# Three edits to a fused attention, soft-MoE and MLP kernel: values' remainder later in the load queue, expert weights two rows per partition, a narrower opening matmul

## The chip, the cores and the metric

The kernel runs on one core of one Trainium2 chip, in float32 with the float32r format in the last stage. The metric is the time of one execution on the device in microseconds. Before the change three runs gave 629.23 to 629.75 us, median 629.69 us. The profiled execution is another one: it took 630.9 us, of which 629.1 us lie between its first and last instruction (the span).

## What is computed

Three layers follow each other, each on the whole output of the one before.

```
# 1. packed attention, 8 batches x 8 heads, 576 tokens of 64, 32 pack queries
p_packed = softmax(p @ k.T / 8) @ v            # 32 x 64 for each head
x = softmax(q @ p_packed.T / 8) @ p_packed     # 576 x 64 for each head, then 4608 x 512
# 2. soft MoE, 8 experts of 4 slots
logits = x @ phi
slots = softmax(logits, over tokens).T @ x     # 32 x 512
slot_out[e] = relu(slots[e] @ w1[e]) @ w2[e]   # w1: 512 x 1024, w2: 1024 x 512
x = softmax(logits, over slots) @ slot_out     # 4608 x 512
# 3. MLP with Mish
out = mish(x @ w_in) @ w_out                   # 512 -> 2048 -> 512
```

The softmax over tokens needs every batch, so the first expert product can't start before the attention of the last batch has ended.

## The kernel before, in words

**Loads.** All loads of q, k, v and of the weights are issued by SyncE (SP), in one order that is fixed when the program is written: the list `jobs` (lines 61 to 214). A job is one load into a named place: a half batch (4 heads) of k or q (576 KB, one DMA), a half batch of v (512 KB, four DMAs of 128 KB, line 129), or 512 KB of weights. `plan` gives each job its place among 29 places for the attention's data, later 37 places of 512 KB; `pump` emits jobs in order, and each DMA waits on SP until the last reader of what lay in its place before is done. SP executes in order, so a load that waits holds up all loads behind it. Up to eight loads of this queue are in flight: each of its DMAs takes the completion semaphore of the one eight DMAs before it and waits for that one to land.

The first 57 jobs, counted from 0, are: k, v, q of batch 0 and k of batch 1 (0 to 7), p (8), then for b = 0, 1, ...: k of batch b+2, v of batch b+1, q of batch b+1, two jobs each. So v of batch 2 is jobs 17 and 18, its q 19 and 20, k of batch 4 is 21 and 22, v of batch 3 is 23 and 24, and so on; k of batch 6 is jobs 33 and 34. Jobs 49 to 56 are the first eight tiles of w_in, and from 57 on come the expert weights, w1 and w2 of four tiles each for every expert, with more w_in tiles among them and sixteen w_out tiles at the end (129 to 144).

**The remainder of v.** A head has 576 = 18 x 32 tokens. Sixteen of the 18 rows of each group of tokens come with job v; the other two, of all eight heads, come as a tile of their own, `vr` (64 partitions, two DMAs of 64 KB in pieces of 256 bytes, line 139), with the second job of that batch's v. There are two buffers of `vr`, so those of batch b wait until the matmuls `pv` of batch b-2 have read theirs.

**Attention.** A loop written out by hand (lines 770 to 817) overlaps three batches: in the pass of b it has the second softmax of b, the product with v of b+1 (`pv`, line 415) and the first softmax of b+2. Each engine executes its instructions in that order. In `pv` the matmuls of a half batch take the sixteen main rows first and the remainder last (line 427).

**Experts.** `ex_h` computes slots @ w1 of an expert, `ex_x` turns its result to put hidden rows on partitions (four matmuls with the 0/1 matrix `idm`, then a 32x32 transpose on VectorE), `ex_o` multiplies with w2. Tile c of w2 holds rows 256c to 256c+255; partition p holds row 256c+p in its first half and row 256c+128+p in its second. The very last tile comes as two DMAs, one for each half. Between the attention and this, the first eight w_in tiles are converted (`bg`), which frees their places for jobs 81 to 93.

**MLP.** 18 blocks of 256 tokens, each in four steps over the hidden dimension. Blocks 5 to 17 form the second product by a scheme with seven products of half size (`emit_o`, lines 1349 to 1368) that add into the PSUM banks Z, V, W, U, X, Y. Bank W holds two sums side by side, 256 columns each. Its first matmul of a block is written over all 512 columns, with a moving operand (`TT["open"]`) whose second half is zeros, so that both halves start from a fresh sum.

Of the kernel before, what the change touches and what calls it, by code (L numbers as in the profile page):

```python
# [9 lines left out]
F32 = mybir.dt.float32  # L10
# [9 lines left out]
def kernel(  # L20
# [13 lines left out]
    nc = tc.nc  # L34
    B, H, S, D = q.shape
    J = p.shape[2]
    E, DM, F1 = w1.shape
    M = phi.shape[1]
# [3 lines left out]
    HQ = H // 4  # L42
# [18 lines left out]
    jobs = []  # L61
# [11 lines left out]
    def plan():  # L73

        late = len(AFTER[E - 1, 1])
        a, x = [("a", i) for i in range(RA)], [("x", i) for i in range(RX)]
        first = [(z, 18 * D * i) for z, n in (("y", 2), ("c", 4), ("w", 16)) for i in range(n)] + a
        order.extend(first[(i - N_QKV) % len(first)] for i in range(N_QKV))
        y, c, w = ([(z, 1024 * i) for i in range(n)] for z, n in (("y", RY), ("c", RC), ("w", RW)))
        again = c[0:1] + w[0:4] + c[1:] + w[8:12] + w[4:8] + w[12:]  # L80
        order.extend((y + c + w + x + a + again + w[0:4] + w[8:12] + w[4:8])[0:len(jobs) - late - N_QKV] + (a + x + a[2:5] + x)[0:late])
# [27 lines left out]
    def take(*name):  # L109
        if name not in got:  # L110
            pump()
        return got[name]
# [10 lines left out]

    vr_t = {}

    def job_v(b, hq):
        def emit(t):
            for h4 in range(4):
                nc.sync.dma_start(
                    out=t[:, 4 * h4 * D:4 * h4 * D + 4 * D],  # L130
                    in_=v[b, 4 * hq + h4].rearrange("(r j) d -> r (j d)", j=18)[:, 0:16 * D].rearrange(
                        "r (a x) -> r a x", a=4,
                    ),
                )
            if hq == HQ - 1:
                vr = t1.tile([64, H, D], F32, name="vr", tag="vr", bufs=2)
                vr_t[b] = vr
                for i in range(2):
                    nc.sync.dma_start(
                        out=vr[32 * i:32 * i + 32], in_=v[b].rearrange("h (r j) d -> r j h d", j=18)[:, 16 + i],  # L140
                    )
        return emit

    def job_w1(e, c):
# [3 lines left out]

    def job_w2(e, c):
        def emit(t):  # L150
            if (e, c) == (E - 1, 3):
                for f in range(2):
                    r = 256 * c + 128 * f
                    nc.sync.dma_start(out=t[:, DM * f:DM * f + DM], in_=w2[e, r:r + 128, :])
                return
            nc.sync.dma_start(
                out=t[:, 0:2 * DM].rearrange("p (f n) -> p f n", f=2),
                in_=w2[e, 256 * c:256 * c + 256, :].rearrange("(f p) n -> p f n", p=128),
            )
        return emit  # L160

# [18 lines left out]
    def add_qkv(nm, b):  # L180
        for hq in range(HQ):
            jobs.append(((nm, b, hq), job_v(b, hq) if nm == "v" else job_kq(k if nm == "k" else q, b, hq)))
# [29 lines left out]
    add_cv((E - 1, 1))  # L212
    assert len([j for j in jobs if j[0][0] in ("wi", "wo")]) == 32
    plan()


    t1 = p1.enter_context(tc.tile_pool(name="t1", bufs=2))
    one = p1.enter_context(tc.tile_pool(name="one", bufs=1))
# [472 lines left out]
    def r_last(b):  # L691
# [13 lines left out]
        out=pT[:, 0:2 * HQ].rearrange("p a c j -> p (a c j)"), in_=p_s.rearrange("p a c -> p (a c)"),  # L705
# [20 lines left out]
        out=pT[:, 2 * HQ:].rearrange("p a c j -> p (a c j)"), in_=take("p")[:, 0:(B - 2) * HQ * D],  # L726
# [223 lines left out]
    for hq in range(HQ):  # L950
        for z in range(2):
            nc.tensor.matmul(
                sit_ps[64 * z:64 * z + 64, 64 * hq:64 * hq + 64].rearrange("p (g m) -> p g m", g=2),
                lhsT=si_acc[:, 64 * hq:64 * hq + 64], rhs=ident.rearrange("p (g z m) -> p z g m", g=2, z=2)[:, z],
                start=True, stop=True,
# [15 lines left out]
    ex = {}  # L971
    idm = t2.tile([128, 512], F32, name="idm", tag="msb")[:, 0:E * (M + SPE)]
    nc.gpsimd.memset(idm, 0.0)
    nc.gpsimd.tensor_copy(
        out=idm.rearrange("p (e x) -> p e x", e=E)[:, :, 0:SPE], in_=ids.rearrange("p (e s) -> p e s", s=SPE),
# [22 lines left out]

    def ex_x(e):

        h1 = ex[e][0].rearrange("p (k c j) -> p k c j", c=4, j=32)
        xp = ps_x.tile([128, FT1, M], F32, name="xp", tag="x")
        for c in range(4):
            nc.tensor.matmul(
                xp[32 * c:32 * c + 32], lhsT=idm[:, M * e:M * e + M], rhs=h1[:, :, c], start=True, stop=True,
            )
        h1T = two.tile([128, FT1, M], F32, name="h1T", tag="h1T")
        nc.vector.transpose(out=h1T.rearrange("p k m -> p (k m)"), in_=xp.rearrange("p k m -> p (k m)"))
        nc.vector.tensor_scalar_max(out=h1T, in0=h1T, scalar1=0.0)
        ex[e][1] = h1T  # L1010
# [71 lines left out]
    ex_h(0)  # L1082
    ex_h(1)
    ex_x(0)
    ex_h(2)
    ex_x(1)
    cb = combine(0)
    next(cb)
    ex_o(0)
    ex_x(2)  # L1090
    ex_h(3)
    ex_o(1)
# [40 lines left out]
    blk = {}  # L1133
# [37 lines left out]
    def fast(n, c):  # L1171

        return not PLAIN.get(n, 0) >> c & 1
# [21 lines left out]
    R = {}  # L1195
# [49 lines left out]
    TT = {}  # L1245

    def wparts(c):
        return whi[:, 4 * c:4 * c + 4], wlo[:, 4 * c:4 * c + 4]
# [70 lines left out]
    def emit_o(n, c, mid):  # L1319

        last = c == ORDER[n][-1]
        H, L = wparts(c)
        x = blk.pop(("g", n, c))

        def mm(bank, o, lhsT, rhs, stop):
            first = (n, bank) not in blk
            blk[n, bank] = True
            nc.tensor.matmul(o, lhsT=lhsT, rhs=rhs, start=first, stop=stop)  # L1328

        mixed = n in PLAIN  # L1330
        if not fast(n, c):
            gh, gl = x
            if (n, c) == (0, 0):
                for w, (g, b, fs) in enumerate(((gh, H, range(4)), (gh, L, range(2)), (gl, H, range(4)), (gh, L, range(2, 4)))):
                    for z, bank in enumerate("XY"):
                        for f in fs:
                            mm(bank, acc(n, bank), g[:, f, 128 * z:128 * z + 128], b[:, f], False)
                    if w > 1:
                        mid(2 * w - 4)
                return  # L1340
            for z, (tt, bank) in enumerate([(0, "X"), (1, "Y")][::-1 if n > 2 and c == ORDER[n][0] else 1]):
                for a, b in ((gh, H), (gh, L), (gl, H)):
                    for f in range(4):
                        mm(bank, acc(n, bank), a[:, f, 128 * tt:128 * tt + 128], b[:, f], last and a is gl and f == 3)
                if not z:
                    mid(0)
                    mid(2)
            return
        gh, gl, Sh, Sl = x
        A = lambda i, j: tuple(g[:, 2 * j:2 * j + 2, 128 * i:128 * i + 128] for g in (gh, gl))  # L1350
        S = lambda k: (Sh[:, k], Sl[:, k])
        Bw = lambda i, j: tuple(w[:, 2 * i:2 * i + 2, 256 * j:256 * j + 256] for w in (H, L))
        T1, T2, T3, T4 = TT[c]
        prods = (
            ("Z", 0, A(0, 0), Bw(0, 0)), ("V", 0, S(1), T2), ("W", 0, S(2), T3), ("X" if mixed else "W", 1, S(3), Bw(1, 1)),
            ("U", 0, S(0), T1), ("Y", 0, A(1, 1), T4), ("X", 0, A(0, 1), Bw(1, 0)),
        )
        for z, (bank, half, (ah, al), (bh, bl)) in enumerate(prods):
            o = R[bank][:, 256 * half:256 * half + 256]
            for f in (1, 0):  # L1360
                if bank == "W" and not mixed and (n, bank) not in blk:
                    mm(bank, R[bank].rearrange("p (z n) -> p z n", z=2), ah[:, f], TT["open"], False)
                else:
                    mm(bank, o, ah[:, f], bh[:, f], False)
                mm(bank, o, ah[:, f], bl[:, f], False)
            for f in (1, 0):
                mm(bank, o, al[:, f], bh[:, f], last and f == 0 and (bank, half) not in (("X", 1), ("W", 2 * mixed)))
            mid(z)
# [116 lines left out]
    for i, (n, c) in enumerate(steps):  # L1485
# [10 lines left out]
        def mid(z):  # L1496
            if z == 0 and last_s:
                nc.scalar.copy(out=quads(n)[1], in_=rq("Z"))
            if z == 1 and last_s:
                add(quads(n)[2], quads(n)[1], rq("V"))  # L1500
            if z in (0, 2) and nx:
                emit_h(*nx, z // 2)
                if i == 0:
                    m = 2 + z // 2
                    blk["mr", m] = bank("XY"[z // 2] + "2")
                    emit_mr(m, blk["mr", m])
# [8 lines left out]
        if i < N0:  # L1515
            cvt(CVT[i][0])
        emit_o(n, c, mid)
        if i == 0:
            cvt("u4 m4")
# [47 lines left out]
```

## Time and profile before

| what | value |
|---|---|
| median of three runs | 629.69 us (629.23 to 629.75) |
| profiled execution, its span | 630.9 us, 629.1 us |
| PE busy | 600.3 us (95%), 5874 matmuls |
| DVE busy | 499.9 us (79%) |
| ACT busy | 339.6 us (54%) |
| POOL busy | 47.9 us (8%) |
| read from HBM, written | 79.23 MB, 9.44 MB |
| chain that ended last | PE 66%, DVE 18%, DMA 8%, ACT 5% |

How to read it: the engines work side by side, so busy shares don't add up to the span, and the span has stages with different limits: attention to about 162 us, experts to about 216 us, the MLP to the end. Matmuls are pipelined, so a busy PE may still be waiting for operands. The chain of waits goes back from the last instruction, at each step to what released it; its shares say which engine the end depended on.

### The profile page before, as it was taken

Reading aid. Unit: us, or ns where it says so; the run is one execution under the profiler, and the core shown is the slowest. Engines: PE = TensorE matmul, PEld = TensorE weight load, DVE = VectorE, ACT = ScalarE, POOL = GpSimd, SP = SyncE. Lnnn points to the kernel's source line nnn. Section 1 sums busy time; section 2 is a strip of 40 time slices with the busy share of each in tenths; the row PEclk is TensorE's granted clock in tenths of the full one; section 3 lists DMA queues with packets and bytes.
Section 4 is the critical chain, followed back from the end, with each engine's and each line's share of the span. In section 5 each row is a group of like instructions: output and inputs, shape, how many; then the busy total and the mean of one; then the engine's idle time right before and its main releaser. Section 6 shows DMA issues by size and latency. Waiting matters only on the chain.

```text
span 629.1 us, 14397 instructions
## 1 busy us (share of the span) xinstructions
PE 600.3 (95%) x5874; PEld 518.4 (82%) x5874; DVE 499.9 (79%) x1004; ACT 339.6 (54%) x684; POOL 47.9 (8%) x73
## 2 busy tenths in 40 slices
PE   7799999998998999999999999999999999999997
PEld 5577777786434468888989899999999999999997
DVE  5998888978464388988999987788778878877883
ACT  3354555447334486666556555555555555555551
POOL 5122222112030000000000000000000000000000
PEclk9999999999999999999999999999999999999999
DMA  8998964999999961002110110111011101110100
GB/s 269 333 323 273 340 226 131 402 407 406 387 410 413 412 260 50 25 0 68 35 34 1 34 35 3 35 34 34 2 34 34 34 2 34 34 29 7 34 34 35
DMA packets 42162, 89.61 MB, mean 142 GB/s; under 512 B 10736, under 2 KB 19056, under 8 KB 42096
## 3 DMA queue, kind: packets, MB, share of 16 engines
q1 hardware_dynamic: 41696, 88.36, 39.5%
q8 instruction: 46, 0.75, 0.5%
q10 hardware_dynamic: 144, 0.26, 0.1%
q14 instruction: 20, 0.16, 0.1%
q0 software_dynamic: 256, 0.07, 0.1%
HBM read 79.23 MB, written 9.44 MB: 141 GB/s over the span
## 4 chain that ended last, share of the span: by engine, by line
PE 66%; DVE 18%; DMA 8%; ACT 5%; issue 1%; SPq 1%; DVEq 0%; POOL 0%; ACTq 0%; POOLq 0%
PE o L1328 45%; PE so L1328 8%; DMA AW<-in_moe_w_dram 7%; PE h L1205 5%; DVE kT L338 4%; DVE A L510 1%; DVE mx L509 1%; PE s L490 1%; DVE AY L1377 1%; DVE S L1221 1%; DVE sm L525 1%; ACT win L356 1%; DMA AC<-in_k_dram 1%; DVE nmx L386 1%; ACT AT L548 1%
## 5 line engine op out<-in xcount | busy, mean ns | idle before, releaser
L1328 PE MATMUL o<-W,gh 128*128 128x256 f32 (+1 forms) x648 | 119.2, 311 | 0.5 <-DVE AY L1377 0.5
L1236 ACT CAST gh<-AY 128x512 fp32r<-128x512 f32 x118 | 54.7, 511 | 111.6 <-PE o L1328 111.6
L1328 PE MATMUL o<-T,Sh 128*128 128x256 f32 x708 | 112.6, 281 | 1.8 <-DVE AY L1377 1.3
L1328 PEld LDWEIGHTS o<-W,gh 128*128 128x128 f32 x648 | 95.2, 188 | 7.8 <-issue 1.3
L1328 PEld LDWEIGHTS o<-T,Sh 128*128 128x128 f32 x708 | 95.7, 188 | 2.9 <-issue 1.1
L1210 ACT ACTIVATE AY<-h 128x512 f32<-128x512 f32 x126 | 74.2, 596 | 24.3 <-PE h L1205 23.3
L1239 DVE TENSOR_TENSOR gl<-AY,gh 128x512 fp32r<-128x512 f32 x118 | 60.5, 554 | 31.5 <-ACT gh L1236 31.5
L1240 DVE TENSOR_TENSOR Sl<-S,Sh 128x1024 fp32r<-128x1024 f32 x59 | 72.2, 1223 | 9.2 <-ACT Sh L1237 9.2
L1328 PE MATMUL o<-W,gl 128*128 128x256 f32 (+1 forms) x324 | 70.6, 310 | 0.0
L1328 PE MATMUL o<-T,Sl 128*128 128x256 f32 x354 | 69.7, 278 | 0.0
L1237 ACT CAST Sh<-S 128x1024 fp32r<-128x1024 f32 x59 | 61.9, 1049 | 7.7 <-DVE S L1221 7.7
L1328 PEld LDWEIGHTS o<-W,gl 128*128 128x128 f32 x324 | 52.4, 188 | 4.0
L1205 PE MATMUL h<-CS,W 128*128 128x256 f32 x288 | 55.4, 281 | 0.0
L1328 PEld LDWEIGHTS o<-T,Sl 128*128 128x128 f32 x354 | 53.8, 188 | 0.0
L1221 DVE TENSOR_TENSOR S<-AY 128x256 f32<-128x256 f32 x118 | 49.6, 420 | 5.2 <-ACT AY L1210 5.2
L1377 DVE TENSOR_TENSOR AY<-AY,o 128x256 f32<-128x256 f32 x115 | 45.1, 418 | 8.6 <-PE o L1328 4.8
L1205 PEld LDWEIGHTS h<-CS,W 128*128 128x128 f32 x288 | 44.0, 188 | 3.1 <-ACT s L1210 0.8
L1328 PE MATMUL so<-W,gh 128*128 128x256 f32 (+1 forms) x268 | 45.9, 294 | 0.0
L1328 PEld LDWEIGHTS so<-W,gh 128*128 128x128 f32 x268 | 37.8, 188 | 2.4 <-ACT W L1191 0.3
L376 PE MATMUL s<-kT,win 128*128 128x288 f32 x128 | 34.7, 414 | 4.7 <-ACT win L388 3.8
L1328 PE MATMUL o<-W,Sh 128*128 128x256 f32 x236 | 36.9, 278 | 0.0
L490 PE MATMUL s<-win,qT 128*128 128x128 f32 x256 | 32.1, 278 | 1.8 <-ACT win L356 1.8
(263 smaller groups left out, 989.2 us busy)
## 6 DMA issues: line engine op xcount, KB each, us to landing
AW<-in_moe_w_dram SPq DMA_DIRECT2D x45, 512.0 KB, 10.1
r_wo<-in_moe_w_out_dram SPq DMA_DIRECT2D x16, 512.0 KB, 8.9
out_dram<-AY SPq DMA_DIRECT2D x64, 128.0 KB, 2.1
r_wi<-in_moe_w_in_dram SPq DMA_DIRECT2D x13, 512.0 KB, 10.3
AW<-in_q_dram SPq DMA_DIRECT2D x11, 576.0 KB, 5.1
AW<-in_k_dram SPq DMA_DIRECT2D x9, 576.0 KB, 7.3
AW<-in_v_dram SPq DMA_DIRECT2D x40, 128.0 KB, 5.5
AC<-in_moe_w_dram SPq DMA_DIRECT2D x10, 512.0 KB, 11.0
```

The source lines that it names most:

```text
L338: nc.vector.transpose(out=T[:, dh, main].rearrange("p (i r a) -> p a i r" if nm == "k" else "p (i a r) -> p a i r", i=4, a=4,), in_=x[:, 0 ...
L376: nc.tensor.matmul(ps[:, n, 0:288], lhsT=pBD[b % 2][:, hq, dh], rhs=kT[:, dh, 288 * n:288 * n + 288], start=(dh == 0), stop=(dh == 1),)
L490: nc.tensor.matmul(ps[:, k - lo], lhsT=d["qT", hq][:, dh, 64 + 128 * i:192 + 128 * i], rhs=ppBD[b % 2][:, hq, dh], start=(dh == 0), stop=( ...
L1205: nc.tensor.matmul(hp[:, 256 * f:256 * f + 256], lhsT=MS[:, 128 * ft:128 * ft + 128], rhs=CS[:, 256 * n:256 * n + 256], start=True, stop=True,
L1210: nc.scalar.activation(out=s, in_=hp.rearrange("p (f n) -> p f n", f=2), func=AF.Mish)
L1221: nc.vector.tensor_tensor(out=S[:, k], in0=x, in1=y, op=op)
L1236: nc.scalar.copy(out=gh[:, f, t], in_=s[:, f, t])
L1237: nc.scalar.copy(out=Sh, in_=S)
L1239: nc.vector.tensor_tensor(out=gl[:, f, t], in0=s[:, f, t], in1=gh[:, f, t].bitcast(F32), op=ALU.subtract)
L1240: nc.vector.tensor_tensor(out=Sl, in0=S, in1=Sh.bitcast(F32), op=ALU.subtract)
L1328: nc.tensor.matmul(o, lhsT=lhsT, rhs=rhs, start=first, stop=stop)
L1377: add = lambda o, x, y: nc.vector.tensor_tensor(out=o, in0=x, in1=y, op=ALU.add)
```

## The change

It has three parts. The two DMAs of `vr` of batches 2 to 7 are issued not with the second v job of that batch but 15 jobs later, just ahead of that job's own DMA; the number of buffers is the same. Tile c of w2 is read with rows 256c+2p and 256c+2p+1 on partition p, 4 KB that lie together in memory, with one DMA also for the last tile; `ex_x` reads the columns of its operand two apart to match. And the first matmul into bank W has 256 columns, as the others.

```diff
+    def load_vr(b):
+        vr = t1.tile([64, H, D], F32, name="vr", tag="vr", bufs=2)
+        vr_t[b] = vr
+        for i in range(2):
+            nc.sync.dma_start(
+                out=vr[32 * i:32 * i + 32], in_=v[b].rearrange("h (r j) d -> r j h d", j=18)[:, 16 + i],
+            )
...
-            if hq == HQ - 1:
-                vr = t1.tile([64, H, D], F32, name="vr", tag="vr", bufs=2)
-                ...
+            if hq == HQ - 1 and b < 2:
+                load_vr(b)
...
     def job_w2(e, c):
-            if (e, c) == (E - 1, 3):
-                for f in range(2):
-                    r = 256 * c + 128 * f
-                    nc.sync.dma_start(out=t[:, DM * f:DM * f + DM], in_=w2[e, r:r + 128, :])
-                return
             nc.sync.dma_start(
-                out=t[:, 0:2 * DM].rearrange("p (f n) -> p f n", f=2),
-                in_=w2[e, 256 * c:256 * c + 256, :].rearrange("(f p) n -> p f n", p=128),
+                out=t[:, 0:2 * DM], in_=w2[e, 256 * c:256 * c + 256, :].rearrange("(p f) n -> p (f n)", f=2),
             )
...
     plan()
-
+    names = [j[0] for j in jobs]
+    for b in range(2, B):
+        i = names.index(("v", b, HQ - 1)) + 15
+        jobs[i] = jobs[i][0], lambda t, b=b, emit=jobs[i][1]: (load_vr(b), emit(t))
...
     def ex_x(e):
-        h1 = ex[e][0].rearrange("p (k c j) -> p k c j", c=4, j=32)
+        h1 = ex[e][0].rearrange("p (k c j f) -> p k f c j", c=4, j=32, f=2)
...
-                xp[32 * c:32 * c + 32], lhsT=idm[:, M * e:M * e + M], rhs=h1[:, :, c], start=True, stop=True,
+                xp[32 * c:32 * c + 32], lhsT=idm[:, M * e:M * e + M], rhs=h1[:, :, :, c], start=True, stop=True,
...
             for f in (1, 0):
-                if bank == "W" and not mixed and (n, bank) not in blk:
-                    mm(bank, R[bank].rearrange("p (z n) -> p z n", z=2), ah[:, f], TT["open"], False)
-                else:
-                    mm(bank, o, ah[:, f], bh[:, f], False)
+                mm(bank, o, ah[:, f], bh[:, f], False)
```

## Rows read from the trace of the kernel before

**Rows 1.** Page, 40 slices of the span: granted clock of TensorE.
```profile
PEclk9999999999999999999999999999999999999999
```

**Rows 2.** Timeline of SP, 33.9 to 62 us: start, us, engine, line, operation, out<-in, count.
```profile
34.06 1.54 SPq L139 DMA_DIRECT2D vr<-in_v_dram  x2
...
46.31 1.03 SPq L139 DMA_DIRECT2D vr<-in_v_dram  x2
...
57.67 1.60 SPq L139 DMA_DIRECT2D vr<-in_v_dram  x2
59.72 0.82 SPq L121 DMA_DIRECT2D AC<-in_q_dram  x2
60.65 0.43 SPq L121 DMA_DIRECT2D AC<-in_k_dram  x1
```

**Rows 3.** DMAs issued from 57.6 to 61.7 us: count, KB each, median us to landing.
```profile
AC<-in_q_dram SPq DMA_DIRECT2D x2, 576.0 KB, 4.9
...
vr<-in_v_dram SPq DMA_DIRECT2D x2, 64.0 KB, 3.1
```

**Rows 4.** Timeline of PE, 44 to 56 us.
```profile
49.02 0.32 PE L428 MATMUL pv<-vr,e1T 64*32 64x64 f32 x8
...
50.57 2.21 PE L376 MATMUL s<-kT,win 128*128 128x288 f32 x8 [0.40 <-ACT win L388]
```

**Rows 5.** Timeline of DVE, 44 to 58 and 73 to 91 us.
```profile
52.44 0.25 DVE L443 STREAM_TRANSPOSE ppT<-pp 128x128 f32<-128x128 f32 x1
...
57.79 0.17 DVE L395 TENSOR_SCALAR r<-sm 128x2 f32<-128x2 f32 x1 [1.71 <-ACT e L388]
...
74.98 0.17 DVE L395 TENSOR_SCALAR r<-sm 128x2 f32<-128x2 f32 x1 [1.71 <-ACT e L388]
```

**Rows 6.** Waits of SP's queue: us in total, times, longest.
```profile
SPq L139 <- PE pv L428: 13.7, 2, 10.2
...
SPq L129 <- DMA AW<-in_k_dram: 6.7, 7, 1.8
```

**Rows 7.** Timeline of SP, 100 to 165 us: waits end and loads go out.
```profile
102.19 0.93 SPq L139 DMA_DIRECT2D vr<-in_v_dram  x2
...
160.94 0.38 SPq L156 DMA_DIRECT2D r_w<-in_moe_w_dram  x1
164.19 0.38 SPq L156 DMA_DIRECT2D AC<-in_moe_w_dram  x1
```

**Rows 8.** Landing times of three single loads, issued at 160.94, 164.19, 233.24 us.
```profile
r_w<-in_moe_w_dram SPq DMA_DIRECT2D x1, 512.0 KB, 8.4
...
AC<-in_moe_w_dram SPq DMA_DIRECT2D x1, 512.0 KB, 6.5
...
r_wo<-in_moe_w_out_dram SPq DMA_DIRECT2D x1, 512.0 KB, 3.6
```

**Rows 9.** Windows: busy us of PE, PEld, DVE, ACT, POOL; PEclk, DMA share, GB/s.
```profile
142.00:162.00 20.00, 16.62 (x243) 12.66 (x232) 15.99 (x44) 12.18 (x36) 3.89 (x6) 1.00 1.03 402
...
192.00:202.00 10.00, 8.57 (x164) 4.56 (x160) 3.35 (x8) 3.53 (x8) 0.00 (x0) 1.00 1.03 416
204.00:213.00 9.00, 8.78 (x122) 4.10 (x122) 2.97 (x8) 3.35 (x7) 0.00 (x0) 1.00 1.05 408
```

**Rows 10.** Chain of waits, 160 to 220 us: start, us, what.
```profile
171.11 0.48 PE xp L1004 x8
...
203.85 10.14 DMA AW<-in_moe_w_dram
```

**Rows 11.** Timeline of PE, 370.4 to 377 us: a 512-column opening and the next step's.
```profile
370.46 0.75 PE L1328 MATMUL o<-T,Sh 128*128 128x512 f32 x4
...
376.00 0.64 PE L1328 MATMUL o<-T,Sh 128*128 128x256 f32 x4
```

**Rows 12.** Line 1328, PE: count, ns min/median/max, first and last start, forms.
```profile
L1328 PE MATMUL o<-T,Sh x708: 276/278/475, 295.7 to 622.8; 128*128 128x256 f32 x164, 128*128 128x512 f32 x13
```

**Rows 13.** Window at the end, columns as in Rows 9.
```profile
624.00:630.00 6.00, 0.66 (x6) 0.47 (x5) 1.14 (x4) 0.00 (x0) 0.00 (x0) 0.77 0.23 87
```

More of the change, by code (lines that the diff above doesn't have):

```diff
@@ L134, in emit @@
                 )
-            if hq == HQ - 1:
-                vr = t1.tile([64, H, D], F32, name="vr", tag="vr", bufs=2)
[L137 to L141, printed above, removed]
+            if hq == HQ - 1 and b < 2:
+                load_vr(b)
         return emit
```

## The prediction, made before the changed kernel ran

> **What bounds the kernel now.** I read the page first, then the chain of waits in order of time, then the timelines of SP, PE and VectorE (DVE) around the edits. The chain has three stretches. Up to 162 us it changes every microsecond or two between DVE, ScalarE (ACT) and PE and hardly ever reaches a DMA: the attention is bound by its own work, one pass of its loop in 17.2 us (the same DVE instruction at 57.79 and 74.98 us [rows 5]). From 172 to 214 us the chain is four loads of expert weights end to end, of which one is shown [rows 10]; the DMA engines are full there, and already in the last 20 us of the attention [rows 9]. From then on it is PE, almost without a gap, to the end. The granted clock is full in every slice [rows 1].
>
> **Remainder of v, the load queue.** In the attention SP waits 13.7 us in two places for `pv` to give back a `vr` buffer, 10.2 us of them before the load of the last batch at 102.19 [rows 6, 7], and all later loads stand behind it. The change takes these waits away. What it puts in their place I get by counting jobs. The second v job of batch 2 is job 18, so its `vr` now goes out ahead of job 33, the first load of k of batch 6. Before, job 33 was issued at 60.65 us [rows 2]. Three pairs of `vr` DMAs no longer stand ahead of it (batches 2, 3, 4): 1.54 and 1.03 us of SP, and 2.05 us from 57.67 to the next issue at 59.72, in all 4.6 us [rows 2]. So `vr` of batch 2 is issued at 56.0 us. Just ahead in the queue are the two halves of q of batch 4, issued 4.6 us earlier than before, at 55.1 and 55.5; such a load lands 4.9 us after its issue [rows 3], the second follows its fellow by about 1 us, and `vr` comes behind both. I estimate its landing at 61.3 us.
>
> `pv` of batch 2 begins its first `vr` matmul at 49.02 us [rows 4]. It will stand for 61.3 - 49.0 = 12.3 us. Behind it on PE are the first softmax of batch 3, which ran at 50.57 after 0.40 us of idling, and all that follows [rows 4]; ACT waits for the result of `pv`, and DVE for ACT, at the transpose that ran at 52.44 [rows 5]. The 0.40 us is slack; after it the delay passes to the pass as a whole: 11.9 us, and I take 11.6.
>
> Bounds for the landing: from the last v of batch 2 to `vr` lie 14 jobs, ten of 576 KB and four of 512 KB, 8.0 MB. At the highest rate that a window shows, 416 GB/s [rows 9], they need 19.2 us; starting at 34.06 us [rows 2] and with the 3.6 us that a load alone takes to land [rows 8] that is 56.9 us, a delay of 7.5 us. If the edit saves no issue time, 60.65 plus the 4.9 us of the loads ahead gives 65.6 us and a delay of 16.2 us.
>
> Can the attention win it back? In a pass DVE idles in one place, 1.71 us [rows 5], for an exponential of ACT that itself waits for DVE, so later passes have no slack to give. Five passes remain; if each gave all of that back, it would be 8.6 us. I take 0, since the wait is inside the loop's own cycle.
>
> The other batches: `vr` of batch 3 comes six jobs later in the queue, about 11 us, so near 72 us; its `pv` is one pass later and delayed as well, near 49 + 17 + 12 = 78 us. It is in time, and later ones have more room, since the queue needs 11.4 us for a batch (from 46.31 to 57.67 [rows 2]) and the attention 17.2. Only batch 2 stalls, once.
>
> **Remainder of v, the experts.** Without the waits the loads run ahead, until they meet places not yet free. Jobs 81 to 93 take places freed by the conversion of w_in at the attention's end, the last of them at 160.94 [rows 7]; their issue moves with the attention, not with the queue. What changes is the backlog: before, the load issued at 160.94 landed after 8.4 us, the one at 164.19 after 6.5 us, while a load with an empty queue takes 3.6 us [rows 7, 8]. The queue will be empty there, so from the load at 164.19 on all land 6.5 - 3.6 = 2.9 us earlier relative to the attention, and the full stretch behind it ends 2.9 us earlier. Bounds: 0, and 8.4 - 3.6 = 4.8 us. The 13.7 us of waits are thus worth 2.9 us.
>
> **w2 in rows of 4 KB.** A stretch of w1 (4 KB rows) moves 416 GB/s, one of w2 (2 KB rows) 408 GB/s, both with full engines [rows 9]. Twenty w2 tiles lie in the full stretch, about 25.7 us of it at 408 GB/s; 2% of that is 0.5 us. Bounds 0 and 0.8 us (all 32 tiles). The strided operand of `ex_x` is not in the trace of before: its eight matmuls of an expert stand with 0.48 us on the chain [rows 10]. Nothing at best, another 0.48 us at worst, and that for the first three experts alone, 1.4 us, as later ones lie beside loads. I take 0, since the stretch after them is the DMA's. Joining the last tile's two DMAs costs nothing: both halves come in 512 KB that land at the same time, and the two products left write different partitions of `so`.
>
> **Narrow opening.** Thirteen matmuls have 512 columns [rows 12]. A group of four with one takes 0.75 us, without 0.64 us [rows 11], so 13 x 0.11 = 1.4 us, on a PE that has no gaps there. Bounds 1.0 and 2.4 us (475 against 278 ns each [rows 12] gives the greater, if all of it stood on PE).
>
> **Clock.** A PE that stands for 12 us is new; the trace shows full clock throughout [rows 1] and a drop to 0.77 in the last window, in which PE is busy for 0.66 of 6 us [rows 13]: an idle PE falls to the lower level, 1.2 GHz. After the stall the 2.21 us of scores [rows 4] and what follows would then take up to twice as long for a while. Bounds 0 and 2.2 us; I take 0.5, as `pv` and the small products around it depend on ACT and DVE more than on columns. The Trainium skill says the same as a warning, "TensorE: Matmul & The Clock Gate", section "Why this matters for your kernels": avoid idle gaps between bursts of matmuls, because one brings the clock back to half rate. By that rule the 2.2 us would fall due in full and the sum would be 1.7 us higher.
>
> **The sum.** 11.6 + 0.5 - 2.9 - 0.5 - 1.4 = +7.3 us. Against the profiled execution, 630.9 us with a span of 629.1, that is 638.2 us; this execution is 1.2 us above the median of the runs, so against 629.69 I forecast 637.0 us. With the ends of the bounds: 7.5 - 4.8 - 0.8 - 2.4 = -0.5, so 629.2 us, and 16.2 + 2.2 + 1.4 - 1.0 = +18.8, so 648.5 us; all ends at once are unlikely.
>
> **Rivals.**
> (A) `vr` of batch 2 is in time, or the wait has cover that I don't see. Then only gains remain: -2.9 - 0.5 - 1.4 = -4.8, 624.9 us, faster. For it: SP's issue times before are stretched by waits for landings [rows 6], which could shrink more than I say. Against: even at 416 GB/s the loads ahead of it end at 56.9 us. It decides at a landing of 49.4 us.
> (B) The attention wins back most of the stall in its idle places, up to 8.6 us: +7.3 - 7 = +0.3, 630 us, about the same. For it: DVE idles in each pass [rows 5]. Against: that idling depends on DVE's own result.
> (C) The queue comes later, and batch 3 is hit too, with the clock low for longer: 16.2 + 2.2 - 4.3 = +14, 643.7 us. For it: the DMA queue waits for landings at every v job [rows 6]. Against: a batch's loads take 11 us and a pass 17.
> (D) The freed waits count in full, 13.7 us, in the experts, and there is no stall: 614 us. Against: places 81 to 93 are freed by the attention [rows 7].
>
> **How the numbers follow.** Forecast 70%, A 10%, B 10%, C 8%, D 2%. The range reaches down to B's 630 and half a microsecond below, and up towards C: 629.5 to 643.0 us. A measurement of this kernel tells 0.2% (1.3 us) from no change. Faster: A and D and a fifth of B, 14%. Same: a third of B and the lowest edge of the forecast, 5%. Slower: the rest, 81%.
>
> **What would show it.** In the timeline of PE one gap of 8 to 16 us between the main and the `vr` matmuls of `pv` near 49 us, released by a DMA into `vr`; SP's wait for `pv` of 13.7 us gone or near it; the end of the attention, at 162 us before, near 174; the load after the first expert's release landing in about 3.6 us; no 512-column form with the moving operand of bank W. Wrong if PE has no gap above 2 us at 49 us, or if the attention's end moves by less than 5 us.

## The result, and the profile after

The changed kernel took 635.36, 636.98 and 638.00 us, median with a fourth run 637.49 us, against 629.72 us (629.23 to 630.3) for the kernel before on the same chip: ratio 1.0102, 95% interval 1.0074 to 1.0131. In every ratio here only those runs of a kernel count that lie within 1.5% of its fastest, so the fourth run, 647.35 us, is left out; experiments 1, 7, 8 and 10 are about what it is. The profiled execution took 635.36 us with a span of 633.6 us, 4.5 us more than the profiled one before.

I matched the two traces matmul by matmul and read how much later each starts after the change: 0.46 us at 48 us, 12.72 us from 68 us to the end of the attention (162.2 became 174.9), 11.44 us from 232 to 345 us, 4.41 us at the end. So the attention loses 12.7, the experts give back 1.3, the MLP gives back 7.0.

The page of the changed kernel, granted clock in 40 slices [rows 1]:

```profile
PEclk9997999999999999999999999999999999999999
```

The timeline of PE after [rows 4]; in brackets the idle time before an instruction and what ended it:

```profile
48.90 0.65 PE L428 MATMUL pv<-AW,e1T 128*32 128x64 f32 x32
60.79 0.43 PE L428 MATMUL pv<-vr,e1T 64*32 64x64 f32 x8 [11.24 <-DMA vr<-in_v_dram]
61.16 1.08 PE L428 MATMUL pv<-AW,e1T 128*32 128x64 f32 x32
...
62.54 3.30 PE L376 MATMUL s<-kT,win 128*128 128x288 f32 x8
```

One gap of 11.24 us, released by the DMA into `vr`. Behind it the same kind of instruction that took 0.65 us takes 1.08, and the scores 3.30 instead of 2.21 [rows 4]: half clock, 1.2 GHz. The windows of the changed kernel (columns as in [rows 9]) say so for the 10.3 us that begin inside the gap. They also show how idle the DMA engines now are from 142 to 162 us, where they were full [rows 9], and that they are full again when the attention ends:

```profile
54.50:64.80 10.30, 4.01 (x53) 2.96 (x54) 1.57 (x4) 1.71 (x6) 1.91 (x4) 0.50 0.99 337
...
142.00:162.00 20.00, 18.06 (x251) 15.00 (x247) 17.31 (x43) 9.39 (x27) 5.30 (x6) 1.00 0.36 112
...
170.00:180.00 10.00, 9.13 (x112) 4.67 (x116) 3.91 (x12) 3.50 (x6) 0.00 (x0) 1.00 1.03 411
```

SP after [rows 2, 7]: `vr` of batch 2 at 54.31, of batch 3 at 65.10 and of the last batch at 114.92; then the two loads of the expert weights whose landing the prediction counted on.

```profile
54.31 0.95 SPq L130 DMA_DIRECT2D vr<-in_v_dram  x2
...
65.10 1.27 SPq L130 DMA_DIRECT2D vr<-in_v_dram  x2
...
114.92 0.33 SPq L130 DMA_DIRECT2D vr<-in_v_dram  x1
...
173.65 0.33 SPq L154 DMA_DIRECT2D r_w<-in_moe_w_dram  x1
176.91 0.33 SPq L154 DMA_DIRECT2D AC<-in_moe_w_dram  x1
```

Their landings, in us after the issue [rows 8]:

```profile
r_w<-in_moe_w_dram SPq DMA_DIRECT2D x1, 512.0 KB, 7.7
...
AC<-in_moe_w_dram SPq DMA_DIRECT2D x1, 512.0 KB, 5.7
```

SP's waits up to 240 us [rows 6]. The wait for `pv` is not gone, 12.7 us instead of 13.7, and a wait for DVE of 12.5 us stands beside it. The longest for `pv`, 11.2 us, is the one ahead of `vr` of the last batch, which goes out at 114.92 us and not at 102.19 [rows 7]: later by 12.7 us, as much as the attention. The wait for DVE ends at 160.38 us, with the first places that the end of the attention frees.

```profile
SPq L130 <- PE pv L428: 12.7, 2, 11.2
SPq L164 <- DVE sm L525: 12.5, 1, 12.5
```

The chain of the changed kernel [rows 10]: the landing of `vr` stands in it once, and the loads of the expert weights take it over at 195 us and hand it to PE at 226.71.

```profile
54.70 5.96 DMA vr<-in_v_dram
...
195.65 9.87 DMA AW<-in_moe_w_dram
205.54 10.84 DMA AW<-in_moe_w_dram
216.44 10.22 DMA AW<-in_moe_w_dram
226.71 1.05 PE so L1016 x4
```

In the MLP no matmul of line 1328 with this operand has 512 columns any more [rows 11, 12]:

```profile
L1328 PE MATMUL o<-T,Sh 128*128 128x256 f32 x708 | 109.7, 277 | 1.9 <-DVE AY L1374 1.5 <-DVE T L1276 0.5
```

That is 1.4 us, as predicted, and not the 7.0 that the stage gives back. The rest is in the spacing. Four windows of the kernel before, each inside one block of the MLP (us, PE busy and in brackets the matmuls that lie in the window, clock, DMA share, GB/s):

```profile
372.00:390.00 18.00, 18.00 (x155) 1.00 0.11 27
394.00:411.00 17.00, 17.00 (x153) 1.00 0.10 25
415.00:433.00 18.00, 18.00 (x155) 1.00 0.10 26
437.00:454.00 17.00, 17.00 (x152) 1.00 0.08 23
```

and the same windows after:

```profile
372.00:390.00 18.00, 18.00 (x161) 1.00 0.13 31
394.00:411.00 17.00, 17.00 (x153) 1.00 0.12 32
415.00:433.00 18.00, 18.00 (x161) 1.00 0.12 31
437.00:454.00 17.00, 17.00 (x152) 1.00 0.13 32
```

The first and third lie in blocks that changed, the second and fourth in blocks that didn't: in 18 us there are 161 matmuls after the change and only 155 before; in 17 us there are 153 and 152 in both. PE is busy all the time and the clock is full. The start times themselves repeat in one of two patterns, a mean of 113.3 ns or of 117.8 ns. Before, blocks of the two kinds alternate (seven of the thirteen at 118 ns, each 0.81 us longer: 5.7 us), and the pattern changes at the 512-column openers; after, it is 113 ns throughout. The page can't show this, since a matmul's own duration, 277 ns, is modelled and pipelined; only the count in a window does.

### The profile page after: what moved, and what is told of

Read it like the earlier page. It is cut to its first block, busy times and chain, and to the rows that moved or that the text cites. A ratio compares the mean times of both kernels' runs of the same rounds, so it can differ in the third digit from the quotient of the medians.

```text
span 633.6 us, 14395 instructions
## 1 busy us (share of the span) xinstructions
PE 594.2 (94%) x5874; PEld 512.3 (81%) x5874; DVE 500.1 (79%) x1004; ACT 339.7 (54%) x684; POOL 47.9 (8%) x73
## 4 chain that ended last, share of the span: by engine, by line
PE 68%; DVE 12%; DMA 11%; ACT 4%; SPq 3%; issue 1%; DVEq 0%; POOL 0%; ACTq 0%; POOLq 0%
PE o L1328 44%; PE so L1328 8%; DMA AW<-in_moe_w_dram 5%; PE h L1205 5%; DVE kT L338 2%; DMA AW<-in_k_dram 2%; SPq L121 2%; PE hp L989 2%; PE so L1016 1%; PE s L490 1%; DVE AY L1374 1%; DMA r_k<-in_k_dram 1%; DMA AY<-in_k_dram 1%; DVE S L1221 1%; DVE A L510 1%
## 5 line engine op out<-in xcount | busy, mean ns | idle before, releaser
L1328 PE MATMUL o<-T,Sh 128*128 128x256 f32 x708 | 109.7, 277 | 1.9 <-DVE AY L1374 1.5
L1328 PEld LDWEIGHTS o<-T,Sh 128*128 128x128 f32 x708 | 93.5, 188 | 2.5 <-DVE AY L1374 1.9
```

## The experiments

All of them run the whole computation. Times are in us; "groups" are the executions of one kernel that lie together. A ratio is that of a kernel to the kernel before. The edits are shown abridged; that of experiment 5 is against the changed kernel, the others against the kernel before.

**1. The narrow opening alone.**

```
-  if bank == "W" and not mixed and (n, bank) not in blk:
-      mm(bank, R[bank] as 2 x 256, ah[:, f], TT["open"], False)
-  else: mm(bank, o, ah[:, f], bh[:, f], False)
+  mm(bank, o, ah[:, f], bh[:, f], False)
```

> The kernel before with the third part alone: the 13 openings of the W bank are 256 columns wide instead of 512. Theory (spacing): in the trace of before the 256-column matmuls start 113 ns apart in some blocks and 118 ns apart in others, and the change from the one to the other falls on the openers; after the change all are 113 ns apart. So the gain is 13 x 0.11 = 1.4 us for the columns and about 7 blocks x 0.81 us = 5.6 us for the spacing: 7.0 us, 622.7 us. Rival: the spacing in the changed kernel came from the later and cooler start of the last stage; then this kernel wins the columns alone, 1.4 us: 628.3 us.

Twelve runs fell into two groups: four at 623.29 to 626.39, eight at 633.05 to 635.15; the kernel before, interleaved with them, 628.75 to 633.43. The first group is near the theory's 622.7 (0.9901, 0.988 to 0.9921), and in its trace the MLP gives back 7.0 us, so the later start was not the cause. The second group, 10 us above, had not been foreseen: about 13 blocks x 0.81 = 10.5 us, a kernel whose blocks all run at 118 ns. No run of that group has a trace, so for this kernel that is an inference. Experiment 7 tests it, and experiment 10's trace, made for another question, shows such a row. The median over all twelve, 633.75, lies above the kernel before.

**2. The larger w2 rows alone** (with the stride in `ex_x` and one DMA for the last tile).

```
-  in_=w2[e, 256c:256c+256].rearrange("(f p) n -> p f n", p=128)
+  in_=w2[e, 256c:256c+256].rearrange("(p f) n -> p (f n)", f=2)
```

> The kernel before with the second part alone: two rows of w2 per partition, the last w2 tile in one DMA, and the stride in the expert's x operand. Theory: the expert stage has only some 20 to 40 us in which it waits for loads, so the larger rows win 0.3 to 0.8 us: 629.2 us. Rival 1: the strided operand costs up to 1.4 us: 631.1 us. Rival 2: the last w2 tile in one DMA instead of two lands later for its first half and takes the gain back: 629.7 us, no change.

629.98 in the median against 630.62, ratio 0.9998 (0.9975 to 1.0020): no difference that can be measured. Its trace gains 0.9 us in the experts, but kernels whose loads are untouched (experiments 6, 7 and 8) differ from the trace of before there by +0.6, -1.3 and -0.1 us. The size of the term stays open within the interval, -1.6 to +1.3 us.

**3. The later remainder of v alone.** The edit of `load_vr` and the lines behind `plan()`, nothing else.

> The kernel before with the first part alone: the remainder of v of batches 2 to 7 is issued 15 jobs later. Theory: the second batch's product stalls 11.2 us, the half clock behind it and the early delay make it 12.7 us at the end of attention, and the experts give back about 1 us of it (what the changed kernel's trace gives back, 1.3 us, less the larger rows): +11.7 us, 641.4 us. Rival (the prediction's term): loads pile up ahead of the experts and 2.9 us come back: +9.8 us, 639.5 us. The spacing of the 256-column matmuls of the last stage may fall otherwise against the 512-column openers, by one or two blocks of 0.81 us either way.

644.57 (643.68 to 647.65), ratio 1.0226 (1.0203 to 1.0249): worse than either expectation. PE of its trace, and the window of its half clock:

```profile
61.40 0.44 PE L434 MATMUL pv<-vr,e1T 64*32 64x64 f32 x8 [12.47 <-DMA vr<-in_v_dram]
61.77 1.08 PE L434 MATMUL pv<-AW,e1T 128*32 128x64 f32 x32
```

```profile
52.40:66.00 13.60, 4.60 (x54) 3.41 (x55) 2.17 (x5) 1.75 (x6) 3.32 (x5) 0.50 0.99 330
```

The gap is 12.47 us, the half clock lasts 13.6, and the attention is 13.6 us late. A second short stretch at half clock near 165 us adds 1.5, which the loads of the experts hide again: at 226 us the lateness is 13.5. So beyond that the loads that ran ahead gave the experts next to nothing here, not 2.9.

**4. The changed kernel without its first part** (experiments 1 and 2 together).

> The changed kernel with its first part undone: the remainder of v is loaded with its own tile, the larger w2 rows and the narrow opening stay. Theory (the parts add): 7.0 us from the opening and 0.5 us from the rows: 622.2 us, which puts the first part at 637.5 - 622.2 = 15.3 us less what it gave back. Rival: the gain of the last stage came only behind the stall; then this kernel stands at 627.8 us (1.4 and 0.5 us).

622.11, 622.23 and 622.63, one at 628.45, and two at 633.13 and 637.18; ratio 0.9887 (0.9852 to 0.9921). The three fastest lie at the theory's sum, 622.2, and the last two fit the second group of experiment 1. Fastest against fastest, 635.36 to 622.11, the first part costs the changed kernel 13.2 us.

**5. Only batches 3 to 7 later,** batch 2 in its old place.

```
-  if hq == HQ - 1 and b < 2:      -  for b in range(2, B):
+  if hq == HQ - 1 and b < 3:      +  for b in range(3, B):
```

> The changed kernel with the remainder of v of batch 2 loaded with its own tile again; batches 3 to 7 stay 15 jobs later, the rows and the narrow opening too. Theory (the stall of batch 2 alone costs the 12.7 us, the later batches are in time): attention ends where it does before, 162 us, and the time is that of the kernel with the second and third part alone, 622.2 us in its faster group of runs. Rival (the stall only shows first in batch 2, and would move to batch 3): batch 3's remainder lands at about 58 us against a need at 66 us by the trace of the changed kernel less 12.7 us; if it lands late, some us of stall at 66 us, 625 us or more.

Eight runs at 630.23 to 634.78 and two at 642.57 and 644.28; ratio 1.0026 (1.0008 to 1.0045), where experiment 4 has 0.9887. The rival holds. The stall moved to batch 3:

```profile
66.21 0.65 PE L428 MATMUL pv<-r_v,e1T 128*32 128x64 f32 x32
72.15 0.44 PE L428 MATMUL pv<-vr,e1T 64*32 64x64 f32 x8 [5.28 <-DMA vr<-in_v_dram]
...
73.90 4.21 PE L376 MATMUL s<-kT,win 128*128 128x288 f32 x8
```

```profile
66.60 0.89 SPq L130 DMA_DIRECT2D vr<-in_v_dram  x2
```

The load goes out at 66.60 and is there at 72.1, which is the prediction's "near 72 us" for batch 3, and my 58 us in the expectation was wrong: I took the 12.7 us of lateness off the queue too, while the queue runs at the transfers' pace whether PE stands or not. In the changed kernel batch 3 was in time only because batch 2 had stalled before it. Gap and half clock (the scores behind it take 4.21 us, not 2.1) make the attention 8.1 us late.

**6. Openers of 512 columns cut in two** of 256, same operands.

> The kernel before with each of the 13 openers of 512 columns cut into two matmuls of 256 columns with the same operands: as many columns as before and 13 instructions more. Theory (the width of the one instruction moves the spacing, not the columns): no block changes its spacing, so 622.7 + 13 x 0.113 = 624.2 us where the row starts at 113 ns, and about 634.7 us where it starts at 118 ns. Rival (the columns, or the zeros, cost it): as before, 629.7 us.

624.78 to 627.84, four runs; ratio 0.9928 (0.9899 to 0.9957). All lie in the theory's first group. The same columns and thirteen instructions more, and still faster than before; in its trace the row stays at 113 ns through all thirteen. So what the opener costs beyond its columns hangs on the single instruction with 512 columns, and the columns and zeros are not it.

**7. One opener of 512 columns,** in the third of the thirteen blocks.

```
-  if bank == "W" and not mixed and (n, bank) not in blk:
+  if bank == "W" and not mixed and (n, bank) not in blk and n == 7:
```

> The kernel before with 256-column openings in 12 of the 13 blocks; one opener of 512 columns stays, in the third of the 13 (392 us in the trace of before). Theory (an opener moves the row of 256-column matmuls from one steady spacing to the other, and what the row starts with is settled by the stall behind the last mixed block, either way in different executions): 113 ns before it and 118 ns behind it, 622.7 + 0.1 + 11 blocks x 0.81 us = 631.7 us, or 118 ns before it and 113 ns behind it, 622.8 + 2 to 2.5 blocks x 0.81 us = 624.7 us; the runs fall into these two groups, and both stay clear of 634. Rival (an opener costs its own block alone, and the two groups of the kernel with 13 narrow openings have another cause): the same two groups as there, 623.5 and 634 us.

Eight runs at 631.16 to 633.84, one at 624.79, three at 635.5 to 636.3; ratio 1.0015 (0.9988 to 1.0041). The first two are the theory's groups; the three lie about 3 us above the mean of the larger one, at a mean granted clock of 0.988 against 0.993 to 1.0. That fits a stretch at half clock as in the last section, but none of the three has a trace. The trace, windows as before:

```profile
372.00:390.00 18.00, 18.00 (x160) 1.00 0.01 3
394.00:411.00 17.00, 17.00 (x147) 1.00 0.01 1
415.00:433.00 18.00, 18.00 (x155) 1.00 0.00 1
437.00:454.00 17.00, 17.00 (x147) 1.00 0.01 1
```

The opener stands at 388.96. Ahead of it 160 matmuls lie in 18 us; behind it 155, and 147 in 17 us instead of 153, and so on to the end. One instruction of 0.2 us costs 9 us, because nothing behind it moves the row back. The rival falls.

**8. Four wide matmuls in a row,** in the second block, three of them multiplying zeros.

```
+  if bank == "W" and not mixed and (n, bank) not in blk and n == 6:
+      mm(bank, w512, ah[:, f], TT["open"], False)
+      for _ in range(3): mm(bank, w512, ah[:, f], zeros_512, False)
```

> The kernel before with 256-column openings, but for one block, the second of the 13, which opens with four 512-column matmuls (three of them multiply zeros, so the result is the same): 4 x 0.21 us in place of 0.11, +0.75 us. Theory (behind several 512-column matmuls the spacing is 113 ns, as behind the plain products at 305 and 329 us in every trace so far): all runs in one group, 622.7 + 0.75 + at most 1.6 us for a slow stretch ahead of it, 623.4 to 625 us. Rival (each 512-column matmul moves the row to the other spacing, so four change nothing): two groups as with 13 narrow openings, 624 and 634.5 us.

Six runs, 624.12 to 627.73, no second group; ratio 0.9907 (0.9884 to 0.9929). This kernel beats the one before and the changed one in every run. That the four wide ones do it isn't shown. By the odds of experiment 1, four in twelve, six in a row would be chance once in 700; but experiment 5 has eight of ten and experiment 6 four of four without them, and by the 23 of 36 runs of all the kernels with narrow openings and no wide ones (the changed one and experiments 1, 4, 5 and 6) it is once in 15. In the trace the row is at 113 ns ahead of the four as well as behind them, as the rival has it too, by which four moves change nothing. The trace also shows the last waits of PE in the MLP at the start of the first block:

```profile
347.30 0.73 PE L1328 MATMUL o<-T,Sh 128*128 128x256 f32 x4 [0.83 <-DVE AY L1380]
...
349.80 0.74 PE L1328 MATMUL o<-T,Sh 128*128 128x256 f32 x4 [0.63 <-DVE AY L1380]
```

They lie ahead of the four wide ones at 369 us. A row that restarts after such a wait can land in either pattern: behind the second of them it runs at 113 ns here and at 118 ns in the trace of before. That fits experiments 1, 4, 5 and 7.

**9. The changed kernel with the four wide ones in the first block.**

> The changed kernel, but the first of the 13 blocks opens with four 512-column matmuls (three multiply zeros), right behind the stall that settles the spacing. Theory (several 512-column matmuls leave the row at 113 ns): all runs in one group, at the changed kernel's 635.4 to 638.0 us plus 0.75 us; none near 647. Rival (the runs near 647 us have another cause, or the first block is too early): two groups 10 us apart.

Two groups: 638.76, and 645.53 to 649.68 (ratio 1.0224, 1.0176 to 1.0272). The theory's one group did not come (the ratio has both groups in it). The rival's second half would explain it, the first block being too early: the four stand right behind the wait at 362.77,

```profile
362.77 1.52 PE L1328 MATMUL o<-T,Sh 128*128 128x512 f32 x7 [0.92 <-DVE AY L1380]
```

and some fifteen matmuls later the spacing in the trace is disturbed once more (146 ns), where the other kernels have their second wait. But four wide matmuls that don't settle the spacing would explain it as well, and the next trace speaks for that. The 10 us between the groups would account for the changed kernel's run at 647.35.

**10. PE kept at work through the stall:** the first half of batch 2's product 30 times over.

> As the kernel with four wide openings in the first block, and TensorE repeats the first half of batch 2's value product 30 times (480 matmuls, about 9.9 us; the last repeat counts) while it waits for the remainder of v. Theory (the half clock from 54.6 to 64.8 us comes from TensorE standing idle): no half clock there, the 64-column matmuls behind the wait take 0.65 us for 32 instead of 1.08, and of the 12.7 us at the end of attention 1 to 1.5 us go: 635.5 us. Rival (the half clock comes by itself, or from the transfers): it stays, the time is that of the kernel without the repeats, 637 us.

671.75 (671.69 to 674.33). The experiment failed by its own weight: each repeat is 32 matmuls in the trace, not 16, and between stretches of 128 to 256 of them PE stood for 1.1 to 4.2 us, six times, 18.3 us in all, with no engine and no load that the profile shows to wait for (`issue`).

```profile
48.33 2.53 PE L424 MATMUL pv<-AW,e1T 128*32 128x64 f32 x163
54.45 5.72 PE L424 MATMUL pv<-AW,e1T 128*32 128x64 f32 x256 [3.59 <-issue]
64.38 3.33 PE L424 MATMUL pv<-AW,e1T 128*32 128x64 f32 x128 [4.21 <-issue]
```

```profile
50.00:60.00 10.00, 6.30 (x315) 5.92 (x304) 1.79 (x6) 0.99 (x3) 4.36 (x6) 0.83 0.92 308
60.00:70.00 10.00, 4.30 (x198) 3.92 (x191) 0.00 (x0) 0.00 (x0) 0.00 (x0) 0.83 0.89 281
```

The product ended at 89 us instead of 62.6. For the question it was made for it says a little: the clock stood at half four times for 3.4 us, at the end of the gaps of 3.6 to 4.2 us, and not for 10 to 14 us in one piece as with a standing PE. That the half clock costs what I put it at is not shown by it.

For experiments 1, 8 and 9 it says more. In the MLP this kernel is experiment 9's, and its four wide matmuls stand at 385.36 us, behind a wait of 0.92 us as there. The windows of 410 to 610 us, first of this trace, then of experiment 9's (columns as in [rows 9]):

```profile
410.00:610.00 200.00, 200.00 (x1700) 200.00 (x1699) 160.11 (x323) 112.06 (x194) 0.00 (x0) 1.00 0.10 27
410.00:610.00 200.00, 200.00 (x1768) 200.00 (x1767) 165.01 (x332) 117.18 (x204) 0.00 (x0) 1.00 0.10 25
```

From 386.37 us to the end the starts lie 117.8 ns apart here and 113.3 there, at full clock in both. Over the 2368 intervals of that row this is 10.5 us: experiment 1's second group, seen in a trace. And the row at 118 ns lies right behind four wide matmuls, so four of them don't always leave 113 ns behind.

**11. The remainder later for batches 6 and 7 alone,** with experiment 9's openers and the larger rows.

> The kernel with four wide openings in the first block, the larger w2 rows, and the remainder of v moved 15 jobs later for batches 6 and 7 alone; in the trace of before only their loads hold the queue (3.6 and 10.3 us on the value product that frees the buffer). Theory: no stall in attention, and the queue runs ahead: 622.2 + 0.75 us, less up to 1.3 us that the experts give back, 621.6 to 623 us in one group. Rival (the freed queue brings nothing, since the experts are not late by these loads): 623.0 us or, if the loads collide with those of attention, 624 us.

621.87 and 621.97, one at 627.06, three at 634.1 to 634.7; ratio 0.9889 (0.985 to 0.9928). No stall, and two groups again. The 621.9 is 0.1 to 0.8 us below the fastest three of experiment 4: too little to tell the theory from the rival.

**12. All batches from 2 on 6 jobs later instead of 15,** otherwise as experiment 9.

> As the changed kernel with four wide openings in the first block, but the remainder of v moves 6 jobs later instead of 15, for all batches from 2 on. Theory (the queue runs at the transfers' pace, about 1.3 us a job up to batch 3, so what is late is counted in jobs): batch 2's remainder is issued at about 41 us and lands at 46 us, 3 us before its use at 49; batch 3's at 53 us, landing at 60 against 66.5: no stall, 622 to 623.5 us. Rival (the delay depends on the traffic ahead, not on the count): a stall of some us at 49 or 66 us, 625 us or more.

621.44, 624.12, 626.27 and 626.65, two near 637; ratio 0.9921 (0.9892 to 0.995). Its timelines, SP and then PE:

```profile
39.90 1.15 SPq L130 DMA_DIRECT2D vr<-in_v_dram  x2
...
51.00 1.93 SPq L130 DMA_DIRECT2D vr<-in_v_dram  x2
```

```profile
48.42 0.32 PE L428 MATMUL pv<-vr,e1T 64*32 64x64 f32 x8
...
65.81 0.32 PE L428 MATMUL pv<-vr,e1T 64*32 64x64 f32 x8
```

Issued at 39.9 and 51.0, expected at 41 and 53, and no gap at either product. With the 54.3 of the changed kernel that is 14.4 us for 9 jobs, 1.6 us a job. The rival's stall did not come; but as the jobs are about equal in size, their count and the traffic ahead go together here, and the two are not told apart. This kernel without wide openings, or with them in the second block, was not run.

## Why the prediction was right, and where it was not

**The stall: right.** Issue forecast at 56.0 us, measured 54.31; landing 61.3, measured before 60.79. The first score behind it starts 11.97 us later than before, of which 0.46 were there before the wait: 11.5 against 11.6. That this agrees so well is partly luck: the wait itself is 11.3 us against 12.3 forecast, less the 0.40 of slack, and the products behind it take 0.6 us more at half clock. Experiments 5 and 12 move the issue by jobs and the stall follows; that is shown. No pass wins anything back: the lateness stays 12.72 us over five passes, so rival B is wrong in its mechanism. For batch 3 the prediction's two numbers, landing near 72 and need near 78, hold (65.10 to about 71, need 79.1), and experiment 5 shows how narrow that was.

**The clock: mis-sized.** 0.5 us forecast; the scores alone take 1.09 us more, of which the slack behind them takes 0.3, so with the 0.6 above it is about 1.4. The 2.2 us that the prediction names as the most did not fall due, because the clock was back at 64.80 us, while the scores still ran; in experiment 5 they did (4.21 us). The other counted runs, at a mean clock of 0.984 against 0.990 for the profiled one, are 1.6 and 2.6 us longer still; which stretches that clock falls in their lack of a trace leaves open. The Trainium skill's warning about idle gaps ("TensorE: Matmul & The Clock Gate", "Why this matters for your kernels") is borne out: the traces show half clock for 10.3 and 13.6 us around gaps of 11.2 and 12.5 us.

**The backlog in the experts: wrong.** "The queue will be empty there" is the step that failed. The loads issued at 173.65 and 176.91 landed after 7.7 and 5.7 us, against 8.4 and 6.5 before, a gain of 0.7 to 0.8 us and not 2.9. DMA was two thirds idle at 142 to 162 us (112 GB/s), but twelve loads of 512 KB go out from 160.38 to 171 us, as places come free at the end of the attention; they fill the queue again (411 GB/s from 170 to 180 us) before the load of 173.65. The step ahead of it, "The change takes these waits away", failed as well: with two buffers `vr` of the last batch still waits for `pv`, 11.2 us until 114.92, and what lead is left ends in the wait for DVE of 12.5 us. With the rows' 0.5 this would be the 1.3 us seen, but that stage differs by -1.3 to +0.6 between kernels with the same loads, so the split is not shown.

**The opening: right in its columns, mis-sized in the whole.** The 13 x 0.11 = 1.4 us are the opener's own; its lasting effect on the matmuls behind it is 5.6 us more. I compared 0.75 with 0.64 us [rows 11] inside one block and never one block with the next, where the counts above differ. (The upper bound there is 13 x 0.197 = 2.6 us, not 2.4; the low end of the sum moves by 0.2.) The gain is -7.0 us in the executions where the row starts at 113 ns, and a loss of about 3.5 where it starts at 118.

**The sum.** Forecast +7.3 on the profiled execution, measured +4.5 there: 12.7 - 1.3 - 7.0 against 12.1 - 3.4 - 1.4. The errors, +0.6 in the attention, +2.1 in the loads and -5.6 in the spacing, partly cancel, and the slower of the other runs bring the median back up to 637.49. The direction rests on the stall, the one term that was right. That the median falls on the forecast is partly luck: had the row started at 118 ns in most of these runs, as in eight of twelve in experiment 1, it would have been near 647.

## What to carry to other kernels

When a load is moved in a queue, count the jobs that it is moved past, give each the time that the transfers need there, and set the landing against the first use of every batch, once with and once without the stall of the batch before it. In a long row of equal matmuls read the number in a window, block by block: two rates under a full clock mean that some other instruction sets the pattern, and a change that removes it fixes the pattern to whatever the row started with. A kernel with two groups of times needs a dozen runs; three may all come from one group.

## What the runs showed of the hardware

Rows of 256-column matmuls of this kernel keep one of two spacings, 113.3 or 117.8 ns at full clock. A single 512-column matmul inside a row moves it from the one to the other nearly every time: in the traces of before and of experiments 2, 3 and 7, at 36 of the 37 that stand behind the first block's waits. A wait of 0.4 to 0.9 us can leave the row in either. Behind rows of twelve 512-column matmuls it was 113 ns in every trace; behind four it was 113 ns in the traces of experiments 8, 9, 11 and 12 and 118 ns in that of experiment 10. What in the engine does this stays open.

Half clock also comes without the edit's stall. In experiment 1's trace TensorE ran at half clock from 158 to 168 us,

```profile
158.00:168.00 10.00, 9.13 (x72) 5.17 (x74) 2.70 (x9) 1.23 (x4) 0.00 (x0) 0.50 0.94 367
```

where 72 matmuls lie instead of 114 before; it cost 4.1 us at 175 us, of which the loads of the experts hid 1.9. Experiment 11's trace has the same stretch. In the 10 us ahead of it PE ran the same matmuls as in the trace of before, which stays at full clock, and waited no longer than 0.6 us at a time in either. Such stretches come in some executions of the same instructions and not in others.
